# Delta attention and a mixture-of-experts MLP on one core: two chunks prepared together, weights loaded and decoded in another order

## The chip, the cores and the metric

The kernel is one program on one core of a Trainium2 chip. The core has TensorE (PE, matmuls and transposes), VectorE (DVE), ScalarE (ACT), GpSimd (POOL) and SyncE (SP, which only issues DMAs here), and 16 DMA engines that move data between HBM (DRAM) and the on-chip memory (SBUF). The metric is the device time of one execution in microseconds (us).

## The reference

Three stages follow one another. 32 heads (4 batches of 8) of a delta rule over 768 steps with head size 48; a squared-ReLU MLP whose weights are float64; and eight experts, of which each of the 3072 rows takes the one that scores best. Cut to what is computed:

```python
# q, k, v (4, 8, 768, 48), beta (4, 8, 768), float32
k_n = k / (np.linalg.norm(k, axis=-1, keepdims=True) + 1e-06)
for t in range(S):                      # 768 steps
    y[:, :, t] = np.einsum('bhd,bhde->bhe', q[:, :, t], state)
    v_old = np.einsum('bhde,bhd->bhe', state, k_n[:, :, t])
    state = state + beta_t * np.einsum('bhd,bhe->bhde', k_n[:, :, t], v_t - v_old)
x = y.transpose(0, 2, 1, 3).reshape(3072, 384)
h = np.maximum(x @ w_in, 0.0)           # w_in  384 x 2048, float64
x = (h * h @ w_out).astype(np.float32)  # w_out 2048 x 384, float64
expert_idx = np.argmax(x @ w_gate, axis=1)           # 8 experts
out[mask] = gate_w[mask] * (np.maximum(x[mask] @ w1[e], 0.0) @ w2[e])   # F = 1024
```

## The kernel before

**Phase 1** goes through the sequence in 12 chunks of 64 tokens (CH). For a chunk c, `pre(c)` loads k and q into the staging tiles st, transposes them into kq (in chunk 1 with matmuls against the identity, in all others with VectorE's block transpose, L359), forms the Gram matrices k k^T and k q^T on TensorE (L370, L371), and sends the key part through DRAM to lay it out anew: gd is written to dg (ScalarE's DMA queue) and read back as gl (SP's queue, L401). From gl come the norms (L440 and the lines behind it), and then a forward substitution inverts one 32x32 triangle per head and half chunk, 31 steps of a multiply (L482) and a subtract (L487). VectorE does each step in two interleaved halves, so that neighbouring instructions do not wait for each other: 120 instructions a chunk. The inverse pt goes out as dt and comes back as tt (L494, L502), again through DRAM.

`chain(c)` then advances the state: u steps (u = tt times the values vz, L547), z steps (what the state already holds is subtracted from vz, L540), y steps (the outputs, written as a high and a low part into xt, L580 and L581), and `s_step`, the update of the state.

The MLP of a chunk is eight units. `l1_unit` is 18 matmuls of 256 columns (L632, two blocks of nine), then ReLU (L636), square, and a split into a high and a low part (the low part on GpSimd, L640). `l2_unit` (L653) runs two units behind it (LAG). `route` picks the experts for the chunk's 256 rows and writes the rows into xs_d. **Phase 2** is the experts, slot by slot, with weights of their own; the change does not touch it.

**The float64 weights** w_in and w_out reach the kernel as pairs of int32 words, lo and hi. They are 14 raw tiles: six of w_in (rawi; 128 rows by 1024 values) and eight of w_out (rawo; 128 by 2 by 384 values), in the order: the three for w_in's first half, two of w_out, the three for w_in's second half, six of w_out. Each is decoded in two halves to float32 in the tile wt: VectorE shifts the exponent and mantissa bits (L141), puts in the sign (L142) and the top bits of lo (L148). The exponent fits float32 only if a value is not too small, so smaller ones are made zero: the hi word loses its sign and is compared with a bound. `DEC` says for each tile where: "b" strips the sign on VectorE (L146), "a" on ScalarE (L144), and both then compare and multiply on VectorE (L153); "s" does it all on ScalarE and GpSimd. At the end the float32 tile is split into high and low parts: a cast on ScalarE (L122) and a subtraction on GpSimd (L123).

**What sets the order.** Every engine works through its instructions in the order in which the code writes them; there is no scheduler. `pre`, `chain`, `update` and `load_weights` are generators, and each `yield` ends a step. Before the main loop the string `ramp` says which step comes next, letter by letter: A a step of chunk 0's `pre`, P one of chunk 1's, C one of chunk 0's `chain`, W a step of the weight decode, L a weight's loads on SP's queue, G the same on GpSimd's, D and E matmuls without a use, Z zeros written to DRAM, B, V, I and q the loads of beta, v and the next k and q. In the main loop every unit has two slots, 16 a chunk, and the tables PRE, CHAIN, LWAT and ROUTE_AT name the slot behind which a step is written:

```python
for n, (c, i) in enumerate(units):
    ...
    pend.append((c, i, l1_unit(c, i)))
    step_bg(NU * c + 2 * i)
    if len(pend) > LAG:
        a = pend.pop(0)
        l2_unit(*a)
    ...
    step_bg(NU * c + 2 * i + 1)
```

By these tables chunk 1's `pre` and `chain`, and the decode of most weights (LWAT), are written into chunk 0's units. `l1_unit` and `l2_unit` call for a weight step themselves if a weight that they need is not there yet.

## Time and profile before

| | |
|---|---|
| median of 3 runs | 1094.23 us (1093.82 to 1100.34) |
| the profiled execution | 1106.22 us, its span 1104.5 us |
| mean granted TensorE clock of that execution | 0.926 of full speed |
| busy, share of the span | TensorE 84%, VectorE 65%, ScalarE 46%, GpSimd 35% |
| first ReLU of chunk 0, 1, 2, 3 | 108.8, 208.3, 274.9, 328.3 us |

The span runs from the first to the last instruction. Busy is the time in which an engine had an instruction at work, issue of DMAs not counted. A stretch of the table's last row lasts from one chunk's first ReLU to the next one's; twelve such marks cut phase 1 into its chunks.

### The profile page before, as it was taken

How to read it: one execution, taken by the hardware profiler on the slowest of the kernel's cores; microseconds unless marked ns; L12 is line 12 of the kernel's file. 1: busy time of each engine (PE TensorE's matmuls, PEld its weight loads, DVE VectorE, ACT ScalarE, POOL GpSimd, SP SyncE). 2: the span in 40 equal slices, each digit the busy share in tenths (PEclk: the TensorE clock that was granted, in tenths of full speed). 3: DMA queues.
4: the chain of work that ended last, by engine and by line, in shares of the span. 5: the costliest groups of instructions: out<-in, count | busy, mean ns of one | idle time of the engine just before them, and what ended most of it. 6: DMA issues, size and time to landing. Idle time of an engine off the chain costs nothing.

```text
span 1104.5 us, 29012 instructions
## 1 busy us (share of the span) xinstructions
...
## 2 busy tenths in 40 slices
...
GB/s 123 117 160 78 127 70 153 12 33 69 61 72 35 76 49 86 35 75 47 84 41 78 48 82 43 42 36 114 131 130 132 258 164 176 222 179 147 215 206 131
DMA packets 284254, 114.22 MB, mean 103 GB/s; under 512 B 252829, under 2 KB 271330, under 8 KB 283712
## 3 DMA queue, kind: packets, MB, share of 16 engines
...
## 4 chain that ended last, share of the span: by engine, by line
PE 54%; DVE 20%; DMA 12%; issue 5%; SPq 4%; ACT 3%; POOL 0%; DVEq 0%; ACTq 0%; POOLq 0%
PE h L632 13%; PE x L653 11%; PE h L1003 6%; PE y L1015 5%; DVE tmp L482 5%; DVE pt L487 4%; PE h L1025 3%; PE y L1035 3%; DVE kq L359 2%; DVE wt L148 2%; DMA dt<-pt 2%; PE u L547 2%; PE wa L1035 2%; DVE wt L142 1%; DMA rawi<-in_moe_w_in_dram 1%
## 5 line engine op out<-in xcount | busy, mean ns | idle before, releaser
L632 PE MATMUL h<-xt,win 128*128 128x256 f32 x1728 | 250.2, 301 | 27.2 <-ACT r L636 11.1
L632 PEld LDWEIGHTS h<-xt,win 128*128 128x128 f32 x1728 | 232.4, 205 | 39.6 <-ACT r L636 11.8
L653 PE MATMUL x<-wout,gt 128*128 128x384 f32 x1152 | 224.8, 343 | 8.1 <-ACT wout L122 5.0
L653 PEld LDWEIGHTS x<-wout,gt 128*128 128x128 f32 x1152 | 198.7, 190 | 14.7 <-ACT wout L122 5.4
L640 POOL TENSOR_TENSOR gt<-r,gt 128x512 fp32r<-128x512 f32 x88 | 114.5, 1301 | 270.3 <-PE x L653 103.2
L482 DVE TENSOR_TENSOR tmp<-pt,gl 128x31 f32<-128x31 f32 (+4 forms) x720 | 153.6, 252 | 3.1 <-DVE pt L487 1.2
L487 DVE TENSOR_TENSOR pt<-pt,tmp 128x31 f32<-128x31 f32 (+4 forms) x720 | 142.8, 237 | 0.8
L636 ACT ACTIVATE r<-h 128x512 f32<-128x512 f32 x96 | 57.4, 598 | 168.1 <-PE h L632 139.3
L917 DVE TENSOR_TENSOR ew<-raw,ew 128x768 fp32r<-128x768 f32 (+1 forms) x98 | 102.5, 1070 | 15.2 <-ACT ew L916 12.7
L379 POOL TENSOR_TENSOR kq<-kq,qmask 64x256 f32<-64x256 f32 x96 | 73.2, 762 | 66.8 <-ACT kq L378 39.4
L916 ACT CAST ew<-raw 128x768 fp32r<-128x768 f32 (+1 forms) x98 | 87.5, 924 | 7.6 <-DMA raw<-in_moe_w_dram 7.6
L1003 PE MATMUL h<-xgT,ew 128*128 128x256 f32 x648 | 83.6, 284 | 7.1 <-issue 6.2
L1003 PEld LDWEIGHTS h<-xgT,ew 128*128 128x128 f32 x648 | 80.5, 191 | 9.5 <-issue 8.6
L1015 PE MATMUL y<-ew,ht 128*128 128x384 f32 x432 | 85.3, 344 | 0.1
...
L370 PE MATMUL gm<-kq 48*64 48x128 f32 (+1 forms) x416 | 60.3, 295 | 21.9 <-DVE kq L359 12.6
L1015 PEld LDWEIGHTS y<-ew,ht 128*128 128x128 f32 x432 | 74.4, 190 | 0.6 <-DVE ht L1007 0.4
L370 PEld LDWEIGHTS gm<-kq 48*64 48x64 f32 x416 | 47.3, 154 | 28.7 <-DVE kq L359 14.5
L359 DVE STREAM_TRANSPOSE kq<-st 64x512 f32<-64x512 f32 x88 | 62.1, 706 | 8.7 <-DMA st<-in_q_dram 7.1
L371 PE MATMUL gm<-kq 48*64 48x128 f32 (+1 forms) x416 | 58.2, 294 | 9.9 <-DVE kq L359 7.6
L1007 DVE SCALAR_TENSOR_TENSOR ht<-h,ht 128x512 fp32r<-128x512 f32 x36 | 24.8, 688 | 61.7 <-ACT ht L1006 53.2
L550 ACT COPY sw<-u 32x384 f32<-32x384 f32 x96 | 45.1, 470 | 41.4 <-PE u L547 39.4
...
## 6 DMA issues: line engine op xcount, KB each, us to landing
...
```

The lines of the kernel that those rows point to most:

```text
L359: nc.vector.transpose(out=kqs[hf][r, x, :, i * CH:(i + 1) * CH].rearrange("p r (u t) -> p r u t", u=2), in_=st[i][r, hf * HP:(hf + 1) * HP],)
L370: nc.tensor.matmul(gm[64:128, j, c0:c1], kq[0:D, 0, r, 0:CH], kq[0:D, 0, r, c0:c1], start=True, stop=True)
L379: nc.gpsimd.tensor_tensor(out=kq[h, x, rs, CH:P], in0=kq[h, x, rs, CH:P], in1=qmask[h].unsqueeze(1).to_broadcast([64, 4, CH]), op=ALU.mult,)
L482: eng.tensor_tensor(out=tv, in0=pt[:, js, s:s + 1].to_broadcast([P, m, n]), in1=gl[:, s:s + 1, s + 1:32].to_broadcast([P, m, n]), op=ALU.mult,
L487: eng.tensor_tensor(out=pt[:, js, s + 1:32], in0=pt[:, js, s + 1:32], in1=tv, op=ALU.subtract)
L632: nc.tensor.matmul(h[:, f2], win_t[kk, half][:, wl, f0:f0 + P], xt[:, xl, kk], start=(n == 0), stop=(n == 3 * KD - 1))
L640: eng.tensor_tensor(out=gt[:, 1], in0=r, in1=gt[:, 0], op=ALU.subtract)
L653: nc.tensor.matmul(x2_t[c][t], gt[:, gl_, f2, ts_], wout_t[i][:, wl, f2], start=(f == 0 and n == 0), stop=(f == NF - 1 and n == 2),)
L916: nc.scalar.copy(dst[:, 0], raw)
L917: nc.vector.tensor_tensor(out=dst[:, 1], in0=raw, in1=dst[:, 0], op=ALU.subtract)
L1003: nc.tensor.matmul(h[:, f2], a[kk][:, wl, f * P:f * P + P], xgT[:, xl, kk, 0:SLOT], start=(n == 0), stop=(n == 3 * KD - 1))
L1015: nc.tensor.matmul(y, ht[:, hl, f2, ts_], b[i][:, wl, f2], start=(f == 0 and n == 0), stop=(f == NF2 - 1 and n == 2),)
```

## The change

**One substitution for chunks 0 and 1.** `pre` is cut into `front` (transposes, Gram matrices of the keys, the way to gl) and `solve` (norms and substitution). `solve((0, 1))` runs the substitution of both chunks together: the two instructions that stand side by side are now chunk 0's and chunk 1's, each over all rows of its triangle, instead of the two halves of one chunk's. `front(0)` and `front(1)` both run ahead of it. The part of the Gram matrices that needs q is a generator of its own, `queries`, with its mask on VectorE. Chunk 1's gl lies in a buffer of xt. Chunks 2 to 11 keep the interleaved halves.

**Transposes.** Chunks 0, 1 and 2 are transposed on TensorE (`turn_in`), and the halves are copied from PSUM by ScalarE and, for x = 1, by VectorE. q of chunks 0 and 1 is staged in buffers of gt.

**Weights.** The decode is three steps of VectorE (shift, sign, low bits). Ahead of it, `lift` multiplies the hi words, read as float32, by 2 to the power of 8 - 119 on ScalarE, in place; this moves the exponent into range and makes small values zero. The weights are 2 to the 8 too large then, and the ReLU and the copy to xr take it out with their scale. The lift of a weight is written one weight ahead of its decode. The list `NEED` names the unit before which each weight is to be ready. The steps of the decode that do not fit ahead of the main loop follow it, in chunk 0's slots.

**Queues.** On SP's queue, weight 0 follows the keys of chunks 0 and 1, the other weights follow gl of both chunks, and none is loaded by GpSimd any more. GpSimd's queue takes q, v and beta of chunks 0 and 1 and half of chunk 0's tt. Chunk 1's CHAIN and chunk 2's PRE now follow the tables of all later chunks. The diff, cut to its core:

```diff
-    DEC="absbbbbabbabbb",
-    ramp="DLLqLLDBWDAAVIDWAWWAWAAAAADLZPAPPAPPPAAACAAAAWAAAWAAPEGWEWWWLLPDPPCPPPGCLCPPPPDCPPPPCPCCPPWWWCWWLGD",
+    ramp="KkqBiVMvLAPAPWaWWAPWaaaaSpWWLLLLLZCSSSSSSSSSSSSSSSSSppppSEEEEEWWWCEEWWWCEEWWWWCEEWWWWCCx",
...
+    NEED=(0, 0, 0, 0, 1, 1, 2.5, 4, 5.5, 7, 8.5, 10, 12, 14),
...
-    TR="dpdddddddddd",
-    WT="ggggrrrrrrrrrr",
+    TR="pppddddddddd",
+    WT="rgrgrgrrrrrrrr",
...
+    LIFT = 8 if wide else 0
+
+    def lift(raw):
+        hf = raw.rearrange("p (f two) -> p f two", two=2)[:, :, 1].bitcast(F32)
+        nc.scalar.activation(hf, hf, AF.Copy, scale=2.0 ** (LIFT - 119))
+
+    def decode(raw, wt):
         pair = raw.rearrange("p (f two) -> p f two", two=2)
         lo, hi = pair[:, :, 0], pair[:, :, 1]
...
-        nc.vector.tensor_scalar(wt, hi, 3, 0x3FFFFFF8, op0=ALU.logical_shift_left, op1=ALU.bitwise_and)
-        nc.vector.scalar_tensor_tensor(wt, hi, -0x40000000, wt, op0=ALU.bitwise_and, op1=ALU.bitwise_or)
-        if way in "ap":
-            nc.scalar.activation(hf, hf, AF.Abs)
-        elif way == "b":
-            nc.vector.tensor_scalar(hi, hi, 0x7FFFFFFF, None, op0=ALU.bitwise_and)
-        yield
+        nc.vector.tensor_scalar(wt, hi, 3, None, op0=ALU.logical_shift_left)
+        nc.vector.scalar_tensor_tensor(wt, hi, -0x80000000, wt, op0=ALU.bitwise_and, op1=ALU.bitwise_or)
         nc.vector.scalar_tensor_tensor(wt, lo, 29, wt, op0=ALU.logical_shift_right, op1=ALU.bitwise_or)
-        if way == "p":
-            nc.gpsimd.tensor_scalar(hf, hf, TINY, None, op0=ALU.is_ge)
-            nc.gpsimd.tensor_tensor(out=wf, in0=wf, in1=hf, op=ALU.mult)
-        elif way != "s":
-            nc.vector.scalar_tensor_tensor(wf, hf, TINY, wf, op0=ALU.is_ge, op1=ALU.mult)
...
+    def load_weights():
+        lifts(0)
+        yield
+        for n, (half, j) in enumerate(order):
+            if n:
+                lifts(n + 1)
+                yield
+            m, ris = halves(n)
...
+                if wide:
+                    decode(ri, wt[:, 0:m])
...
+                yield
...
+            for i in range(2):
+                split(t, i, wf[i])
+            yield
+            if n == 0:
+                lifts(1)
                 yield
...
+        vt, eng = vz[c % 2], (nc.gpsimd if c < 2 else nc.sync)
...
+                (nc.gpsimd if c < 2 and i else nc.sync).dma_start(out=tv[r0:r0 + 64], in_=head_view(a, par, c * CH, CH))
...
+    def turn_in(c, i):
+        kqs = kqb[c % 2]
+        src = src_t[c, i]
+        for g in range(4):
+            tp = ps_a.tile([P, 4, P], F32, tag="a", name="tp")[0:64]
+            hf, js = g // 2, slice(4 * (g % 2), 4 * (g % 2) + 4)
+            for j in range(4):
+                r = 4 * g + j
+                nc.tensor.transpose(tp[:, j], src[:, r * D:r * D + 64], ident)
+            for x in range(2):
+                to, by = kqs[hf][64 * x:64 * x + 64, x, js, i * CH:(i + 1) * CH], tp[:, :, 64 * x:64 * x + 64]
+                if (c < 2 and i == 0 or c == 2) and x:
+                    nc.vector.tensor_copy(to, by)
+                else:
+                    nc.scalar.copy(to, by)
...
+    def solve(cs):
+        w = 32 * len(cs)
+        gls = [gl_t.pop(c) for c in cs]
...
+        both = len(cs) > 1
...
+            for h in range(2):
+                js, m = (slice(0, nj), nj) if both else (slice(h, nj, 2), (nj + 1 - h) // 2)
+                if m:
+                    ops.append((gls[h * both], pts[h * both], js, m, tmp[:, h, 0:m * n].rearrange("p (a b) -> p a b", a=m)))
...
+                        (nc.gpsimd if c == 0 and x else nc.sync).dma_start(out=tt[r0:r0 + 32, u], in_=dtr[hf, x, u])
...
-        nc.scalar.activation(r, h, AF.Relu)
+        nc.scalar.activation(r, h, AF.Relu, scale=2.0 ** -LIFT)
...
-            nc.scalar.copy(xr, x2p[t])
+            nc.scalar.activation(xr, x2p[t], AF.Copy, scale=2.0 ** -LIFT)
...
-                nc.sync.dma_start(out=bl[r0:r0 + 32], in_=bf[:, :, u, :])
+                nc.gpsimd.dma_start(out=bl[r0:r0 + 32], in_=bf[:, :, u, :])
...
+    step = {"A": f0, "P": f1, "S": p01, "C": ch, "u": update(0), "W": lw, "a": qs[0], "p": qs[1]}
```

What the instructions of three places look like before and after, in the program's order; the number behind a tile's name is its buffer's.

**VectorE, the substitution, the fifth of the 31 steps and half of the sixth.** tmp is the product, pt the inverse that grows. Before, one chunk (pt_375, gl_283), each instruction over every second row:

```order
L482 TENSOR_TENSOR tmp_393<-pt_375,gl_283 128x54
L482 TENSOR_TENSOR tmp_393<-pt_375,gl_283 128x27
L487 TENSOR_TENSOR pt_375<-pt_375,tmp_393 128x2x27
L487 TENSOR_TENSOR pt_375<-pt_375,tmp_393 128x27
L482 TENSOR_TENSOR tmp_393<-pt_375,gl_283 128x52
L482 TENSOR_TENSOR tmp_393<-pt_375,gl_283 128x26
```

After, chunk 0 (pt_455, gl_400) and chunk 1 (pt_456, gl_403):

```order
L503 TENSOR_TENSOR tmp_566<-pt_455,gl_400 128x81
L503 TENSOR_TENSOR tmp_566<-pt_456,gl_403 128x81
L508 TENSOR_TENSOR pt_455<-pt_455,tmp_566 128x3x27
L508 TENSOR_TENSOR pt_456<-pt_456,tmp_566 128x3x27
L503 TENSOR_TENSOR tmp_566<-pt_455,gl_400 128x78
L503 TENSOR_TENSOR tmp_566<-pt_456,gl_403 128x78
```

The same places hold instructions of 81 and 78 elements for each of two chunks, where they held 54 and 27, 52 and 26 for one.

**VectorE, the decode of a w_out tile.** Before, five instructions for a half, two halves:

```order
L141 TENSOR_SCALAR wt_1153<-rawo 128x384
L142 SCALAR_TENSOR_TENSOR wt_1153<-rawo,wt_1153 128x384
L146 TENSOR_SCALAR rawo<-rawo 128x384
L148 SCALAR_TENSOR_TENSOR wt_1153<-rawo,wt_1153 128x384
L153 SCALAR_TENSOR_TENSOR wt_1153<-rawo,wt_1153 128x384
```

After, from the last step ahead of a decode that stands in the ramp (a z step) over the two halves of the tile:

```order
L570 TENSOR_TENSOR vz_134<-vz_134,z 128x384
L130 TENSOR_SCALAR wt_901<-rawo 128x384
L131 SCALAR_TENSOR_TENSOR wt_901<-rawo,wt_901 128x384
L132 SCALAR_TENSOR_TENSOR wt_901<-rawo,wt_901 128x384
L130 TENSOR_SCALAR wt_901<-rawo 128x384
L131 SCALAR_TENSOR_TENSOR wt_901<-rawo,wt_901 128x384
L132 SCALAR_TENSOR_TENSOR wt_901<-rawo,wt_901 128x384
```

L146 and L153 are gone from VectorE, and nothing writes to rawo there.

**SP's queue around dt, the way of pt through DRAM.** Before, from the loads of chunk 1's v (vz_141) and k (ktok) to chunk 1's gl:

```order
L314 DMA vz_141<-in_v_dram 32x8x32
L295 DMA ktok_643<-in_k_dram 64x16x48 x2
L494 DMA dt_226<-pt_375 1024x1x32 x2
L502 DMA tt_722<-dt_226 32x8x32 x8
L401 DMA gl_731<-dg_445 64x1024 x2
L178 DMA rawo<-in_moe_w_out_dram 128x768 x2
```

After, from weight 0 to chunk 0's tt:

```order
L157 DMA rawi<-in_moe_w_in_dram 32x2048 x4
L415 DMA gl_400<-dg_207 64x1024 x2
L415 DMA gl_403<-dg_237 64x1024 x2
L157 DMA rawi<-in_moe_w_in_dram 32x2048 x4
L157 DMA rawi<-in_moe_w_in_dram 16x2048 x8
L157 DMA rawo<-in_moe_w_out_dram 128x2x768 x2
L157 DMA rawi<-in_moe_w_in_dram 32x2048 x8
L157 DMA rawi<-in_moe_w_in_dram 16x2048 x8
L273 DMA ktok_563<-in_k_dram 64x16x48 x2
L518 DMA dt_691<-pt_455 1024x1x32 x2
L518 DMA dt_694<-pt_456 1024x1x32 x2
L528 DMA tt_697<-dt_691 32x8x32 x4
```

Seven weights and ktok stand between gl of both chunks and dt; before, ktok alone stood right ahead of it, and chunk 1's gl behind tt.

## Rows read from the trace of the kernel before

**Rows 1.** Busy time of each engine (instructions) by stretch, PEclk, DMA share, GB/s.

```profile
0.00:108.80 108.80, 44.29 (x750) 36.50 (x754) 78.69 (x322) 31.99 (x79) 39.06 (x64) 0.76 0.71 119
108.80:208.30 99.50, 59.82 (x730) 54.36 (x731) 88.54 (x126) 39.55 (x86) 51.11 (x52) 0.73 0.50 99
208.30:274.90 66.60, 57.44 (x816) 51.46 (x815) 52.31 (x227) 29.13 (x66) 18.81 (x19) 0.88 0.31 45
274.90:328.30 53.40, 51.75 (x800) 46.94 (x800) 33.77 (x140) 28.70 (x64) 18.20 (x18) 0.99 0.46 70
328.30:755.60 427.30, 401.86 (x6253) 371.05 (x6252) 290.40 (x1276) 209.94 (x459) 139.92 (x136) 0.98 0.36 56
```

**Rows 2.** Timeline of ScalarE: chunk 0's and chunk 3's first ReLU.

```profile
108.77 0.60 ACT L636 ACTIVATE r<-h 128x512 f32<-128x512 f32 x1 [1.39 <-PE h L632]
...
328.34 0.60 ACT L636 ACTIVATE r<-h 128x512 f32<-128x512 f32 x1 [2.91 <-PE h L632]
```

**Rows 3.** Chain that ended last, start and length, from 143 us.

```profile
143.09 1.37 DVE rawi L146
144.46 1.69 DVE wt L148
```

**Rows 4.** Groups by line and shape, first 210 us.

```profile
L632 PE MATMUL h<-xt,win 128*128 128x256 f32 x162 | 31.4, 365 | 18.7 <-ACT r L636 11.1 <-DVE xt L581 4.4 <-ACT win L122 1.9
...
L146 DVE TENSOR_SCALAR rawo<-rawo 128x384 int32<-128x384 int32 x14 | 13.4, 960 | 0.5
L153 DVE SCALAR_TENSOR_TENSOR wt<-rawo,wt 128x384 f32<-128x384 f32 x16 | 11.8, 738 | 0.7
L359 DVE STREAM_TRANSPOSE kq<-st 64x512 f32<-64x512 f32 x16 | 11.3, 705 | 7.5 <-DMA st<-in_q_dram 7.1
...
L153 DVE SCALAR_TENSOR_TENSOR wt<-rawi,wt 128x512 f32<-128x512 f32 x10 | 7.3, 726 | 0.6
...
L146 DVE TENSOR_SCALAR rawi<-rawi 128x512 int32<-128x512 int32 x6 | 5.0, 834 | 0.2
...
L144 ACT ACTIVATE rawi<-rawi 128x512 f32<-128x512 f32 x4 | 2.7, 684 | 14.4 <-DVE wt L142 14.4
```

**Rows 5.** VectorE on the tile wt, first 210 us.

```profile
0.00:210.00 210.00, 78.88 (x110) 0.75 0.60 109
```

**Rows 6.** Timeline of VectorE: five places in chunk 0's substitution.

```profile
37.81 0.19 DVE L482 TENSOR_TENSOR tmp<-pt,gl 128x31 f32<-128x31 f32 x1
...
39.75 0.29 DVE L482 TENSOR_TENSOR tmp<-pt,gl 128x29 f32<-128x29 f32 x2
39.98 0.29 DVE L487 TENSOR_TENSOR pt<-pt,tmp 128x29 f32<-128x29 f32 x2
...
45.29 0.36 DVE L482 TENSOR_TENSOR tmp<-pt,gl 128x72 f32<-128x72 f32 x2
45.56 0.35 DVE L487 TENSOR_TENSOR pt<-pt,tmp 128x72 f32<-128x72 f32 x2
```

**Rows 7.** Chain that ended last, first 140 us.

```profile
31.45 0.27 ACT s L440
...
65.62 0.58 SPq L494
...
71.62 5.36 DMA tt<-dt
...
112.24 13.03 DMA rawi<-in_moe_w_in_dram
```

**Rows 8.** Timeline of TensorE: chunk 0's first u step and first layer-1 matmul.

```profile
81.71 1.58 PE L547 MATMUL u<-vz,tt 32*32 32x48 f32 x64
...
96.51 0.38 PE L632 MATMUL h<-xt,win 128*128 128x256 f32 x1 [0.46 <-ACT xt L580]
```

**Rows 9.** Timeline of GpSimd: two of its DMA issues.

```profile
36.73 0.83 POOL L788 DMA_DIRECT2D wg<-in_moe_w_gate_dram  x1
...
38.57 0.62 POOL L793 DMA_DIRECT2D xs_d<-zrow  x1
```

315 lines of the change are left out of this document (148 added, 167 removed).

## The prediction

> **What bounds the kernel now.** I read the stretches first. Cut at the first ReLU of each chunk, a settled chunk takes 53.4 us: TensorE is busy 51.75 of chunk 2's 53.4, VectorE 33.8, and the eight chunks from 328.3 on average the same 427.3/8 [rows 1]. The change leaves that part and all that follows alone, so what it can win lies before chunk 3's first ReLU, at 328.34 [rows 2]. Three stretches lie there: 108.8 us up to chunk 0's first ReLU, 99.5 us for chunk 0 and 66.6 us for chunk 1. In chunk 0's 99.5 us TensorE is busy 59.8 and VectorE 88.5, so VectorE sets the pace. The chain of waits says with what: the weight decode, whose 128x384 steps are long at this place (L146 1.37 us, L148 1.69) [rows 3]. The groups by line and shape say what one step costs on average there [rows 4]. In the first stretch nothing is full, VectorE 78.7 of 108.8 and the DMA engines 0.71 [rows 1]: it is a path of dependent steps, and I price it as a path.
>
> **The decode.** 28 weight halves are decoded. L146 (the sign stripped on VectorE) is 13.4 + 5.0 us and L153 (tiny values flushed) 11.8 + 7.3 us [rows 4]: together 37.5 us leave VectorE. The three steps that stay write wt, as L153 does; VectorE works on wt for 78.9 us in 110 instructions [rows 5], and without L153's 26 that is 59.8 us for 84, or 2.14 us a half. These are means with GpSimd at work beside them, as it will be again. In exchange ScalarE lifts all 28 halves, at L144's 0.684 us at most 19 us [rows 4]. Its own queue is in order, so a lift that waits for its load holds up every ReLU behind it; that is the second rival.
>
> **One substitution for two chunks.** The 31 steps are 120 instructions a chunk now, in two interleaved halves, and 124 for both chunks afterwards, each on a whole triangle row. Two instructions of 29 elements take 0.23 us from start to start and the two of 72 and 54 take 0.27 [rows 6]: 0.04 us for 68 more elements, so some 0.6 ns an element over 0.098 us an instruction. Both chunks have 4 x 2856 elements, which gives 124 x 0.098 + 11424 x 0.0006 = 19 us; were all of the longer pair's 0.27 us for 126 elements to grow with the elements, it would be 24. I take 20, and 3 more for the stalls beside GpSimd. From the square root (31.45) to the first step (37.81) it is 6.4 us [rows 6, 7]; a second scaled gl and two more clears add some 3. Were the solve to start at 31.5 as before, it would end at 31.5 + 9.4 + 23 = 64, against 65.6 for chunk 0 alone now [rows 7]. So chunk 1's solve costs the first stretch almost nothing.
>
> **The path to the first ReLU.** Then pt goes out and comes back as tt. Now that takes from 65.62 to the landing of tt at 71.62 + 5.36 = 77.0, 11.4 us [rows 7]. By VectorE alone tt would be there at 64 + 11.4 = 75.4. But dt now stands in SP's queue behind seven more weights and ktok. By the shapes in the code 13.3 MB are to move before it: 7.9 of weights 0 to 7, 2.4 of k, q and v, 1.6 of dg and gl, 0.9 of zeros, 0.5 of beta and ktok. The first 108.8 us move 119 GB/s at a share of 0.71, 168 GB/s while busy [rows 1], which makes 79 us; the large packets of weights 6 and 7 with ktok (2.5 MB) took 13.0 us [rows 7], 191 GB/s, which makes 70. I take 73 and 8 more for dt and tt, so tt at 81 (bounds 75 and 89). From u's first matmul to the first layer-1 matmul it is 96.51 - 81.71 = 14.8 us now [rows 8]; decoding weights 3 and 4 lies in that stretch and fits beside u, the copies and y, and I leave it at 14 to 15. A layer-1 unit of 18 matmuls takes 31.4/9 = 3.5 us at that clock [rows 4]. Now 12.3 us pass between the first layer-1 matmul and the first ReLU, because weights 1 and 2 are not split; afterwards they are decoded while tt is in flight. First ReLU: 81 + 14.3 + 3.5 = 98.8 against 108.8. **Gain 10** (2 to 16).
>
> **Chunk 0.** Nine weights are left, 18 halves x 2.14 = 38.5 us of VectorE. A settled chunk's other work is 33.8 [rows 1]. Of it the transposes of one chunk go (8 x 0.705 = 5.6 [rows 4]) and eight copies from PSUM come (no row; between 0.3 and 0.6, by the 0.29 to 0.36 of small steps [rows 6] and the 0.705 of a transpose; I take 0.35, 2.8 us), and 9 us of chunk 2's solve fall into chunk 1's stretch by the table. That is 60 us. At the share that VectorE reaches now, 88.5 of 99.5, it takes 67; without any idle time 60. TensorE has 51.75 less the two second-layer units that lag, plus 32 transposes: about as much, at a clock that was 0.73 here [rows 1] and may stay under 1. I take 64. **Gain 35.5** (27 to 40).
>
> **Chunk 1.** A settled 53.4, and 9 us more VectorE work, which fits in the 19.6 us that VectorE idles: 55. **Gain 11.6** (6 to 13).
>
> **What costs nothing.** GpSimd takes over q, v and beta of chunks 0 and 1 and half of chunk 0's tt: 48 DMAs stand ahead of the first u step in its queue. An issue of 128 pieces took 0.62 us there and one of 384 took 0.83 [rows 9], some 1 ns a piece, so the four of 1024 pieces take about 1.5 and all 48 some 36 us, with 6 of memsets and splits 42: hidden until 81. If that cover is gone, see the third rival. The relu's and the copy's scale ride on instructions that are there. TensorE's 64 transposes for chunks 0 and 1 replace 64 smaller matmuls and VectorE's transposes, while TensorE mostly waits.
>
> **Sum.** 10 + 35.5 + 11.6 = 57 us off the profiled execution's 1106.2 (its span is 1104.5) is 1049. The median of the three runs, 1094.2, lies 12 us below that execution; the gain is in the same stretch for both, so I forecast **1037**.
>
> **Rivals.** First: the DMA engines rule the start. If they move no more than the 119 GB/s that the first stretch averages, 13.3 MB take 112 us, tt is there at 120 and the first ReLU comes at 138, 29 us later than now; chunks 0 and 1 still give 47, net 18, so 1076. For it: the share is 0.71 with VectorE waiting; against it: by the code's shapes k and q of chunk 0 come in pieces of 64 and 128 bytes now and of 192 afterwards, weights 0 to 2 in pieces of 4 KB and then of 8. Second: chunk 0 stays uneven, because lifts, splits and ReLUs share ScalarE's queue. Its 39.6 us of chunk 0 [rows 1] become some 52: lifts and splits of the remaining weights (about 20) on a settled chunk's 28.7, and 3 of copies. If every unit waits 2 us for a lift, chunk 0 takes 80 and the time is 1053. Third, the other side: GpSimd's queue. All of chunk 0 hangs on its tt, behind those 48 DMAs. At x us each tt lands at 48x + 10; up to 1.5 us nothing is lost, and from 2.7 us on (tt at 140) the whole gain is gone. At 3.1 us tt lands at 159, 78 us late, and the time is 1115. Both issues in rows 9 were made while VectorE ran the substitution, and took 0.62 and 0.83.
>
> The Trainium skill speaks for this rival: its page "SBUF — State Buffer" says under "SBUF: two separate sides" that a DMA issued by GpSimd waits for its descriptors while VectorE holds the port they share, and under "A bandwidth-pool intuition that's wrong (but worth ruling out)" gives 3.1 us in place of 0.62. By that figure the time would be the 1115 above. The trace disagrees here, with 0.62 and 0.83 us beside a busy VectorE [rows 9].
>
> **How the numbers follow.** Forecast, 1020 to 1050: 0.60. ScalarE's queue, about 1053: 0.15. DMA, about 1076: 0.10. GpSimd, 1100 and more: 0.04. Better than forecast, with tt at 75 and chunk 0 bound by TensorE at 55, about 1018 or less: 0.09. Little or nothing, because a wait that I don't see takes the place: 0.02. The range is 1013 to 1066: it takes in the first two and the better case, and leaves out DMA and what is slower. Within 1% (1083 to 1105) is about what a measurement of this kernel can't tell from no change. Faster by more: the forecast, ScalarE, the better case and most of the DMA case, 0.92; within 1%: 0.04; slower: 0.04.
>
> **What would show it.** In the new profile: the joint substitution ends before 70 us; tt lands between 75 and 89, with dt issued late if the weights hold it; the first ReLU comes at 93 to 105, chunk 1's 60 to 70 us later, chunk 3's between 258 and 282, and from there to the end nothing changes; VectorE's busy time falls by 40 to 60 us, ScalarE's rises by 5 to 15. I am wrong if chunk 0's stretch stays over 80 us with VectorE under 75% busy, which would say that the decode was not what paced it, or if GpSimd's DMA issues at the start take over 1.5 us each.

## The result and the profile after

| | before | after |
|---|---|---|
| median of 4 runs | 1097.06 us (1093.82 to 1100.34) | 1053.30 us (1052.08 to 1055.59) |
| the profiled execution, span | 1106.22, 1104.5 us | 1052.59, 1050.8 us |
| first ReLU of chunks 0, 1, 2, 3 | 108.8, 208.3, 274.9, 328.3 us | 101.5, 175.4, 227.0, 282.4 us |

The ratio is 0.9603, with a 95% interval of 0.9562 to 0.9645: 43.8 us faster by the medians, where 57 were forecast. The predicted time, 1037 us, is 16 us below the measured one, inside the stated range.

Busy time by stretch after the change, cut at the same marks as [rows 1] (from:to, length, then busy time and instructions of TensorE's matmuls and weight loads, VectorE, ScalarE and GpSimd, then clock, DMA share and GB/s):

```profile
0.00:101.50 101.50, 50.44 (x736) 36.28 (x740) 69.87 (x235) 28.84 (x68) 43.43 (x70) 0.71 0.94 194
101.50:175.40 73.90, 54.07 (x778) 48.44 (x776) 62.01 (x126) 45.60 (x105) 41.05 (x36) 0.85 0.26 43
175.40:227.00 51.60, 50.77 (x800) 46.02 (x799) 33.84 (x147) 28.79 (x64) 17.31 (x18) 1.00 0.37 58
227.00:282.40 55.40, 52.07 (x801) 47.77 (x800) 40.49 (x177) 28.87 (x65) 19.24 (x19) 0.95 0.41 66
282.40:708.70 426.30, 402.73 (x6252) 373.54 (x6252) 291.60 (x1264) 210.09 (x459) 139.84 (x136) 0.97 0.35 56
```

The marks are the ReLUs that answer to [rows 2]; the timeline of ScalarE:

```profile
101.50 0.60 ACT L668 ACTIVATE r<-h 128x512 f32<-128x512 f32 x1 [6.14 <-PE h L664]
...
282.38 0.60 ACT L668 ACTIVATE r<-h 128x512 f32<-128x512 f32 x1 [7.41 <-PE h L664]
```

Read against [rows 1], stretch by stretch:

| stretch | before | after | gain | forecast |
|---|---|---|---|---|
| to chunk 0's first ReLU | 108.8 | 101.5 | 7.3 | 10 |
| chunk 0 | 99.5 | 73.9 | 25.6 | 35.5 |
| chunk 1 | 66.6 | 51.6 | 15.0 | 11.6 |
| chunk 2 | 53.4 | 55.4 | -2.0 | 0 |
| chunks 3 to 10 | 427.3 | 426.3 | 1.0 | 0 |
| from chunk 11's first ReLU to the end | 348.9 | 342.1 | 6.8 | 0 |

The four stretches that the change touches give 45.9 us where 57 were forecast. The last row is chunk 11 and phase 2, which the change all but leaves alone: its length differed from profile to profile in all the kernels below, between 341.0 and 349.8 us, and the 6.8 us in that row are of that kind. Chunks 3 to 10 took between 420.5 and 431.4 us there.

What happens at the start shows on SP's queue (start, time until the last issue of the row, queue, line, transfer and count):

```profile
54.10 17.58 SPq L157 DMA_DIRECT2D rawi<-in_moe_w_in_dram  x10
71.73 1.35 SPq L273 DMA_DIRECT2D ktok<-in_k_dram  x2
73.18 4.35 SPq L518 DMA_DIRECT2D dt<-pt  x4
78.44 5.78 SPq L528 DMA_DIRECT2D tt<-dt  x12
```

and on VectorE, where the first and the last steps of the joint substitution answer to [rows 6]:

```profile
40.30 0.29 DVE L503 TENSOR_TENSOR tmp<-pt,gl 128x31 f32<-128x31 f32 x2
...
60.77 0.30 DVE L508 TENSOR_TENSOR pt<-pt,tmp 128x16 f32<-128x16 f32 x2
```

The inverse is ready at 61.1, but its transfer is issued at 73.2, behind ten pieces of weights that SP's queue gave out between 54.1 and 71.7: the 73 of the prediction, and a wait of 12 us.

In chunk 0 the decode is the reading to make. VectorE on the tile wt, in the first two stretches:

```profile
0.00:101.50 101.50, 22.41 (x36) 4.37 (x8) 10.07 (x8) 0.71 0.94 194
101.50:175.40 73.90, 42.71 (x48) 9.88 (x20) 23.41 (x20) 0.85 0.26 43
```

48 instructions are 16 halves, so a half costs 2.67 us in chunk 0, against 2.14 forecast from [rows 5]; in the first stretch it is 22.41/12 = 1.87. Undisturbed, the three steps of a 128x512 half take 0.42, 0.69 and 0.69 us (at 70 us). VectorE's busy time in chunk 0, 62.0, is nevertheless near the 60 of the prediction. But the stretch is 73.9 and not 64: VectorE stands idle for 11.9 us of it, most of them in one wait at the start, behind ScalarE's half of the copies of chunk 2's transposes.

```profile
108.68 1.41 DVE L329 COPY kq<-tp 64x256 f32<-64x256 f32 x4 [7.75 <-ACT kq L331]
```

TensorE, busy for 54.1 us, stands still in two large holes. TensorE's timeline, with the idle time before the instruction and what ended it:

```profile
149.53 2.97 PE L566 MATMUL z<-sw,kq 96*32 96x48 f32 x64 [7.42 <-ACT sw L580]
...
169.21 0.58 PE L664 MATMUL h<-xt,win 128*128 128x256 f32 x1 [5.74 <-ACT xt L610]
```

Both wait for a small copy on ScalarE, and this is what stands ahead of the copies there:

```profile
148.06 0.93 ACT L116 CAST wout<-wt 128x384 fp32r<-128x384 f32 x2 [2.17 <-DVE wt L132]
149.00 1.95 ACT L580 COPY sw<-u 32x384 f32<-32x384 f32 x4
...
167.86 0.92 ACT L116 CAST wout<-wt 128x384 fp32r<-128x384 f32 x2 [6.61 <-DVE wt L132]
168.69 0.47 ACT L610 CAST xt<-y 128x384 fp32r<-128x384 f32 x1
```

A cast that waits for VectorE's decode keeps the next chunk's small copies (of its state, L580, and of its outputs, L610) waiting behind it, and TensorE with them.

### The profile page after: what moved, and what is told of

The parts are those of the page before. It is cut to its first block, busy times and chain, and to the rows that moved or that the text cites. A ratio compares the mean times of both kernels' runs of the same rounds, so it can differ in the third digit from the quotient of the medians.

```text
span 1050.8 us, 28874 instructions
## 1 busy us (share of the span) xinstructions
PE 921.1 (88%) x11416; PEld 857.7 (82%) x11416; DVE 673.4 (64%) x2234; ACT 511.6 (49%) x1025; POOL 382.4 (36%) x388
## 5 line engine op out<-in xcount | busy, mean ns | idle before, releaser
L664 PE MATMUL h<-xt,win 128*128 128x256 f32 x1728 | 245.0, 297 | 26.5 <-DVE xt L611 15.7
L664 PEld LDWEIGHTS h<-xt,win 128*128 128x128 f32 x1728 | 226.8, 201 | 35.2 <-DVE xt L611 18.1
L672 POOL TENSOR_TENSOR gt<-r,gt 128x512 fp32r<-128x512 f32 x88 | 114.1, 1296 | 277.7 <-ACT gt L670 101.4
L685 PEld LDWEIGHTS x<-wout,gt 128*128 128x128 f32 x1152 | 201.6, 193 | 9.1 <-issue 3.7
L503 DVE TENSOR_TENSOR tmp<-pt,gl 128x60 f32<-128x60 f32 (+37 forms) x662 | 146.4, 259 | 2.4 <-DVE tmp L503 0.4
L508 DVE TENSOR_TENSOR pt<-pt,tmp 128x60 f32<-128x60 f32 (+37 forms) x662 | 133.0, 239 | 0.7
L942 ACT CAST ew<-raw 128x768 fp32r<-128x768 f32 (+1 forms) x98 | 87.6, 923 | 11.9 <-DMA raw<-in_moe_w_dram 11.9
L1041 PEld LDWEIGHTS y<-ew,ht 128*128 128x128 f32 x432 | 74.8, 191 | 0.1
L390 POOL TENSOR_TENSOR kq<-kq,qmask 64x256 f32<-64x256 f32 x80 | 60.1, 751 | 35.6 <-issue 18.8
L580 ACT COPY sw<-u 32x384 f32<-32x384 f32 x96 | 45.1, 470 | 38.1 <-PE u L577 36.2
L669 ACT ACTIVATE r<-r 128x512 f32<-128x512 f32 x96 | 60.7, 632 | 3.0
L670 ACT CAST gt<-r 128x512 fp32r<-128x512 f32 x96 | 59.6, 621 | 5.1 <-ACT r L669 0.4
L1069 POOL DMA_INDIRECT out_dram<-yo,ids x30 | 33.5, 1117 | 70.0 <-DMA out_dram<-yo,ids 21.1
L381 PE MATMUL gm<-kq 48*64 48x128 f32 (+1 forms) x384 | 49.1, 268 | 6.4 <-DVE kq L370 6.2
```

Of the source, the lines that this page charges most:

```text
L390: nc.gpsimd.tensor_tensor(out=kq[h, x, rs, CH:P], in0=kq[h, x, rs, CH:P], in1=qmask[h].unsqueeze(1).to_broadcast([64, 4, CH]), op=ALU.mult,)
L503: nc.vector.tensor_tensor(out=tv, in0=pt[:, js, s:s + 1].to_broadcast([P, m, n]), in1=gl[:, s:s + 1, s + 1:32].to_broadcast([P, m, n]), op ...
L508: nc.vector.tensor_tensor(out=pt[:, js, s + 1:32], in0=pt[:, js, s + 1:32], in1=tv, op=ALU.subtract)
L664: nc.tensor.matmul(h[:, f2], win_t[kk, half][:, wl, f0:f0 + P], xt[:, xl, kk], start=(n == 0), stop=(n == 3 * KD - 1))
L669: nc.scalar.activation(r, r, AF.Square)
L670: nc.scalar.copy(gt[:, 0], r)
```

## The experiments

Four theories went in. **V**: VectorE's decode paces chunk 0. **P**: the gain comes from preparing both chunks ahead, not from the decode. **Q**: ScalarE's queue, worked through in order, paces chunk 0. **D**: SP's queue of weights sets tt. The medians of before differ by chip (1095.5 to 1103.5 us), so the ratio to before on the same chip is what compares; first ReLU and chunks are from each kernel's profile.

| kernel | ratio, 95% interval | median | first ReLU | chunk 0 | chunk 1 |
|---|---|---|---|---|---|
| changed kernel | 0.9603, 0.9562 to 0.9645 | 1053.3 | 101.5 | 73.9 | 51.6 |
| e1_old_decode | 0.9747, 0.9669 to 0.9824 | 1067.5 | 103.1 | 87.5 | 56.0 |
| e2_new_decode_alone | 1.0019, 0.9974 to 1.0063 | 1098.9 | 124.8 | 76.8 | 69.3 |
| e3_weights_behind_tt | 0.9514, 0.9434 to 0.9594 | 1045.1 | 92.4 | 73.7 | 52.0 |
| e4_no_gpsimd_split | 0.9455, 0.9378 to 0.9533 | 1038.1 | 101.4 | 63.0 | 57.6 |
| e5_lift_in_place | 0.9947, 0.9911 to 0.9984 | 1094.2 | 106.2 | 92.2 | 65.5 |
| e6_copies_on_scalar | 0.9681, 0.9626 to 0.9736 | 1067.6 | 105.1 | 74.8 | 52.0 |
| e7_weights_needed_later | 0.9583, 0.9515 to 0.9651 | 1057.3 | 104.9 | 70.4 | 57.8 |
| e8_two_substitutions | 0.9705, 0.9641 to 0.9769 | 1068.8 | 112.9 | 74.1 | 54.6 |
| e9_casts_ahead | 0.9600, 0.9507 to 0.9692 | 1061.3 | 107.0 | 72.1 | 56.3 |
| e10_all_three | 0.9515, 0.9431 to 0.9600 | 1051.0 | 92.9 | 73.1 | 53.4 |
| e11_low_part_unread | 0.9639, 0.9583 to 0.9695 | 1057.1 | 101.7 | 74.0 | 54.4 |
| e12_masks_on_vector | 0.9553, 0.9494 to 0.9611 | 1045.7 | 91.1 | 77.1 | 54.6 |

### The change without its decode, and the decode without the rest

**e1_old_decode.** On the changed kernel:

```diff
-    LIFT = 8 if wide else 0
+    LIFT = 0
...
-        nc.scalar.activation(hf, hf, AF.Copy, scale=2.0 ** (LIFT - 119))
...
+        nc.vector.tensor_scalar(wt, hi, 3, 0x3FFFFFF8, op0=ALU.logical_shift_left, op1=ALU.bitwise_and)
+        nc.vector.scalar_tensor_tensor(wt, hi, -0x40000000, wt, op0=ALU.bitwise_and, op1=ALU.bitwise_or)
+        nc.vector.tensor_scalar(hi, hi, 0x7FFFFFFF, None, op0=ALU.bitwise_and)
         nc.vector.scalar_tensor_tensor(wt, lo, 29, wt, op0=ALU.logical_shift_right, op1=ALU.bitwise_or)
+        nc.vector.scalar_tensor_tensor(wt.bitcast(F32), hi.bitcast(F32), TINY, wt.bitcast(F32), op0=ALU.is_ge, op1=ALU.mult)
```

> The changed kernel with the old decode: five steps on VectorE for every weight half (sign stripped and tiny values flushed there), no lift on ScalarE, no scale in the ReLU. Theory V (chunk 0 is paced by VectorE's decode): 12 halves stand ahead of the first ReLU and 16 behind it, each longer by 1.6 to 1.7 us; the first ReLU comes 5 to 8 us later than 101.5, chunk 0 takes 93 to 100 us in place of 73.9, and the time is 1078 to 1088 us. Theory P (what the change won came from preparing both chunks ahead and from the order, not from the decode): chunk 0 stays under 82 and the time under 1063. Theory Q (ScalarE's queue, in order, with the lifts in it, paces chunk 0): without lifts chunk 0 gets no longer, 1048 to 1056.

Busy time by stretch, first and second:

```profile
0.00:103.10 103.10, 51.13 (x736) 36.65 (x740) 80.68 (x257) 22.66 (x57) 43.82 (x70) 0.73 0.93 195
103.10:190.60 87.50, 58.36 (x778) 51.95 (x775) 79.36 (x160) 38.01 (x89) 40.94 (x36) 0.78 0.20 31
```

VectorE is busy 17.4 us longer in chunk 0 (79.4 against 62.0), the chunk takes 13.6 us longer and the next one 4.4. The time lies between the bands of V and P; Q in this form is out, for ScalarE lost its lifts and nothing got shorter. The first ReLU, which V had 5 to 8 us later, came 1.6 later, though VectorE's work ahead of it grew by 10.8 us (69.9 to 80.7): the start hangs little on the decode. The rest of the change without the decode gives 2.5% (by the interval 1.8 to 3.3), and the decode on top of it 1.4%.

**e2_new_decode_alone.** On the kernel before; decode and scales as in the change, and in `weight`:

```diff
+        if n == 0:
+            lift(0)
+        lift(n + 1)
         raw = raw_t.pop(n)
```

> The kernel before with nothing changed but the decode: three steps, the lift one weight ahead, the scales in ReLU and copy. Theory V: VectorE's 88.5 us in chunk 0 fall by 20 to 28, chunk 0's 99.5 us to 72 to 80, the first ReLU moves by less than 5, the time is 1069 to 1077 us against 1097. Theory P: chunk 1's preparation, a chain of dependent steps, still fills chunk 0; chunk 0 stays over 90 and the time is 1087 to 1097.

Busy time by stretch, and ScalarE's lift of weight 3:

```profile
0.00:124.80 124.80, 41.85 (x746) 34.51 (x750) 73.10 (x319) 32.06 (x80) 38.45 (x67) 0.76 0.70 122
124.80:201.60 76.80, 52.99 (x731) 48.51 (x732) 63.66 (x81) 45.51 (x99) 46.49 (x42) 0.83 0.48 100
```

```profile
94.84 0.55 ACT L141 ACTIVATE rawo<-rawo 128x384 f32<-128x384 f32 x1 [22.05 <-DMA rawo<-in_moe_w_out_dram]
```

Chunk 0 has the length that theory V gave it, 76.8 for 99.5. But the first ReLU comes 16 us later, because a lift waited 22 us for its weight in ScalarE's queue, with the square root and the state's copies behind it, so the chunk ends, at chunk 1's first ReLU, only 6.7 us earlier (201.6 for 208.3). Alone, the new decode wins nothing.

**e5_lift_in_place.** As e2, with the lift inside `decode`, right ahead of its first step:

```diff
+        nc.scalar.activation(hf, hf, AF.Copy, scale=2.0 ** (LIFT - 119))
         nc.vector.tensor_scalar(wt, hi, 3, None, op0=ALU.logical_shift_left)
```

> The kernel before with the three-step decode, as in e2, but each half's lift written right ahead of its own decode and not one weight ahead; nothing else is changed. In e2 chunk 0 fell from 99.5 to 76.8 us, and the first ReLU came 16 us later, because a lift in ScalarE's queue waited 22 us for weight 3. If that wait is the whole cause: the first ReLU comes at 106 to 112, chunk 0 takes 74 to 82, and the time is 1070 to 1080 us against 1095. If lifts as such hold up ScalarE wherever they stand (theory Q): the first ReLU stays later than 115 or chunk 0 over 85, and the time is 1085 to 1097.

```profile
0.00:106.20 106.20, 43.59 (x746) 36.28 (x750) 69.04 (x314) 30.99 (x77) 36.18 (x62) 0.59 0.70 122
106.20:198.40 92.20, 58.97 (x729) 53.67 (x730) 61.42 (x88) 47.25 (x102) 49.69 (x52) 0.74 0.54 107
```

Two of VectorE's waits for a lift:

```profile
110.69 1.78 DVE L138 TENSOR_SCALAR wt<-rawo 128x384 int32<-128x384 int32 x1 [3.10 <-ACT rawo L137]
116.54 1.08 DVE L138 TENSOR_SCALAR wt<-rawo 128x384 int32<-128x384 int32 x1 [2.89 <-ACT rawo L137]
```

The start is as expected (106.2), chunk 0 is not: it and the time lie in the bands of Q. VectorE's busy time in it fell by 27 us, 88.5 to 61.4 [rows 1], and the chunk by 7.3. So VectorE's work alone does not pace it. In place of the work came waits: VectorE waited 13 times for a lift in this chunk, 23.1 us in all, and never in e2, where 61 to 64 us of the same work took 76.8 us and not 92.2. Part of that difference is where chunk 0 is taken to begin: its end, chunk 1's first ReLU, comes at 198.4 here and at 201.6 in e2. Either way theory V in its plain form falls.

### The start

**e3_weights_behind_tt.** One edit of the table: the loads of weights 5 to 7 are written behind dt and tt.

```diff
-    ramp="KkqBiVMvLAPAPWaWWAPWaaaaSpWWLLLLLZCSSSSSSSSSSSSSSSSSSppppSEEEEEWWWCEEWWWCEEWWWWCEEWWWWCCx",
+    ramp="KkqBiVMvLAPAPWaWWAPWaaaaSpWWLLZCSSSSSSSSSSSSSSSSSSLLLppppSEEEEEWWWCEEWWWCEEWWWWCEEWWWWCCx",
```

> The changed kernel with the loads of weights 5, 6 and 7 written behind dt and tt on SP's queue instead of ahead. If the queue of weights holds dt (theory D): the substitution ends at 61, dt is issued by 63 in place of 73.2, tt has landed by 73 in place of 83, the first ReLU comes at 90 to 93 in place of 101.5, and the time is 1042 to 1046 us. If tt is not what the first ReLU waits for (decode of weights 3 and 4, the state chain on ScalarE), or if the three weights then come too late, the first ReLU stays within 3 us and the time at 1050 to 1056.

SP's queue, and busy time by stretch:

```profile
42.08 12.06 SPq L273 DMA_DIRECT2D ktok<-in_k_dram  x2
61.61 2.88 SPq L518 DMA_DIRECT2D dt<-pt  x4
65.50 5.79 SPq L528 DMA_DIRECT2D tt<-dt  x12
71.34 8.51 SPq L157 DMA_DIRECT2D rawi<-in_moe_w_in_dram  x13
```

```profile
0.00:92.40 92.40, 49.57 (x740) 35.14 (x744) 73.44 (x235) 29.20 (x68) 44.35 (x70) 0.76 0.91 161
92.40:166.10 73.70, 52.84 (x778) 47.13 (x773) 61.79 (x124) 45.60 (x104) 41.11 (x36) 0.88 0.45 108
```

Theory D holds: dt is issued at 61.6 in place of 73.2, the first ReLU comes 9.1 us earlier, chunk 0 keeps its length, and the three weights are still early enough. The two later kernels with this edit, e10 and e12, repeat it (92.9 and 91.1).

**e8_two_substitutions.** On e3:

```diff
-    ramp="KkqBiVMvLAPAPWaWWAPWaaaaSpWWLLZCSSSSSSSSSSSSSSSSSSLLLppppSEEEEEWWWCEEWWWCEEWWWWCEEWWWWCCx",
+    ramp="KkqBiVMvLAPAPWaWWAPWaaaaSpWWLLZCSSSSSSSSSSSSSSSSSLLLSSSSSSSSSSSSSSSSSppppEEEEEWWWCEEWWWCEEWWWWCEEWWWWCCx",
...
-    f0, f1, p01, ch = front(0), front(1), solve((0, 1)), chain(0)
...
+    f0, f1, p01, ch = front(0), front(1), two(), chain(0)
...
+    def two():
+        yield from solve((0,))
+        yield from solve((1,))
```

> The kernel of e3 (weights 5 to 7 behind tt, 1045 us) with two substitutions one after the other, chunk 0's and then chunk 1's, each in its two interleaved halves, in place of the joint one; dt and tt of chunk 0 are issued after the first. By the prediction's price the joint one takes 20 us for both and a single one some 15 to 17: the first ends near 56 and tt lands 4 to 6 us earlier than in e3, but VectorE is at the second until 74 to 78, and the decode of weights 1 and 2 and the first z step come behind it. First ReLU 93 to 100 in place of 92.4, time 1046 to 1053. If tt alone sets the first ReLU: 86 to 90, time 1039 to 1043. If the joint substitution is what the change lives on: 105 or later, over 1057.

VectorE, the wait in the middle of the first substitution:

```profile
53.29 0.96 DVE L491 TENSOR_TENSOR vz<-vz,ncol 128x768 f32<-128x768 f32 x1 [10.30 <-ACT ncol L489]
```

and ScalarE around it:

```profile
52.01 1.19 ACT L125 ACTIVATE rawi<-rawi 128x512 f32<-128x512 f32 x2 [11.21 <-DMA rawo<-in_moe_w_out_dram]
53.10 0.15 ACT L489 COPY ncol<-nps 128x16 f32<-128x16 f32 x1
```

112.9 against e3's 92.4 (and 92.9 in e10, on the same chip) is, by the number, the third case of the expectation, but 10.3 us of it are something that I had not seen in my own edit: a single substitution scales vz by the norms at its tenth step, and the copy of the norms stood on ScalarE behind a lift that waited 11.2 us for its weight. The joint one does the norms after its last step. Without the 10.3 the first ReLU would be near 102.6, an estimate between the first case and the third, and about 10 us are left for the joint substitution itself. So the run bears out that it is worth that much, and not cleanly.

### Chunk 0

**e4_no_gpsimd_split.** The subtraction that forms the weights' low part is left out:

```diff
-        nc.gpsimd.tensor_tensor(out=dst[:, 1, n], in0=raw, in1=dst[:, 0, n], op=ALU.subtract)
...
-                    nc.tensor.matmul(h[:, f2], win_t[kk, half][:, wl, f0:f0 + P], xt[:, xl, kk], start=(n == 0), stop=(n == 3 * KD - 1))
+                    nc.tensor.matmul(h[:, f2], win_t[kk, half][:, 0, f0:f0 + P], xt[:, xl, kk], start=(n == 0), stop=(n == 3 * KD - 1))
...
-                        x2_t[c][t], gt[:, gl_, f2, ts_], wout_t[i][:, wl, f2],
+                        x2_t[c][t], gt[:, gl_, f2, ts_], wout_t[i][:, 0, f2],
```

> The changed kernel without GpSimd's subtraction that forms the weights' low part; the matmuls that read the low part read the high part in its place, so the product is less exact. GpSimd loses 28 of its instructions of 1.1 to 1.3 us. Theory V with contention (GpSimd's own work beside a decode step stretches it): a half's decode in chunk 0 falls from 2.67 us to 2.1 or less, chunk 0 from 73.9 to 63 to 68, the time to 1043 to 1048. Theory Q (the casts and copies in ScalarE's queue pace it, whatever VectorE takes): decode at 2.67, time 1050 to 1056.

Busy time in chunk 0, of all instructions and then of those on wt:

```profile
101.40:164.40 63.00, 51.20 (x778) 46.37 (x775) 49.18 (x123) 45.35 (x105) 17.81 (x16) 0.91 0.34 62
```

```profile
101.40:164.40 63.00, 32.62 (x48) 9.87 (x20) 0.91 0.34 62
```

A half's decode falls to 32.62/16 = 2.04 us and chunk 0 by 10.9, as theory V with contention expected; chunk 1 gives 6 back. The time, 1038.1, is below the 1043 of that theory: by the ratios this kernel is some 16 us faster than the changed one, of which the two stretches show 4.9, and the rest is not placed. What this kernel leaves out is more than exactness: the high part stands in for the low one and counts twice, so h comes out about twice as large. The matmuls' number and shapes are the same.

**e11_low_part_unread.** Of e4 only what the matmuls read: GpSimd subtracts, and nothing on TensorE waits for it.

> The changed kernel in which GpSimd still forms the weights' low part, but no matmul reads it (they read the high part in its place, as in e4, so the product is less exact). GpSimd's work is that of the changed kernel; only TensorE's waits for it are gone. It splits what e4 won: chunk 0 there took 63.0 us in place of 73.9, at 2.04 us a half's decode in place of 2.67. If GpSimd's work beside VectorE stretches the decode (contention): 2.6 to 2.7 us a half as in the changed kernel, chunk 0 at 71 to 74, and 0.958 to 0.962 of the time before. If TensorE's waits for the low part are what e4 took away: chunk 0 at 63 to 66, and 0.945 to 0.950.

Chunk 0, all instructions and those on wt:

```profile
101.70:175.70 74.00, 51.92 (x777) 46.82 (x773) 63.20 (x128) 45.62 (x104) 41.09 (x36) 0.86 0.28 53
101.70:175.70 74.00, 43.84 (x50) 9.88 (x20) 23.45 (x20) 0.86 0.28 53
```

Chunk 0 stays at 74.0, and a half's decode at 2.63 us (43.84 for 50 steps, three to a half). What e4 took away is GpSimd's work itself, not TensorE's waits for it. How GpSimd's work reaches VectorE shows in one pair of rows of the changed kernel, VectorE's and GpSimd's (a subtraction for the ReLU's low part, of the same operation and size as those for w_in):

```profile
119.06 1.79 DVE L132 SCALAR_TENSOR_TENSOR wt<-rawi,wt 128x512 int32<-128x512 int32 x1
```

```profile
119.04 1.27 POOL L672 TENSOR_TENSOR gt<-r,gt 128x512 fp32r<-128x512 f32 x1 [0.56 <-ACT gt L670]
```

GpSimd starts 0.02 us earlier and is done at 120.31; VectorE's step, 0.69 us when undisturbed, is done at 120.85, 0.54 behind it. It waited out nearly the whole instruction. In e11 the same two instructions take 1.78 and 1.27 us, and VectorE's is again done 0.54 us behind.

**e6_copies_on_scalar.** VectorE stands idle for 7.8 us at the start of chunk 0 behind a copy of chunk 2's transposes; these copies go to ScalarE.

```diff
-                if (c < 2 and i == 0 or c == 2) and x:
+                if c < 2 and i == 0 and x:
```

> The changed kernel with the eight copies of chunk 2's transposes that VectorE makes moved to ScalarE; chunks 0 and 1 keep theirs. In the changed kernel VectorE stands idle for 7.8 us at the start of chunk 0, behind such a copy, with the decode of weight 6 next in its queue. Theory V (VectorE's queue paces chunk 0, its waits count in full): the idle time is gone, chunk 0 falls from 73.9 to 66 to 69 us, the time to 1045 to 1049. Theory Q (ScalarE's queue): 8 x 0.36 us more on ScalarE, chunk 0 gets 0 to 3 us longer, 1053 to 1057.

Busy time in chunk 0, and what VectorE does in the place of that wait:

```profile
105.10:179.90 74.80, 53.87 (x778) 47.69 (x771) 60.53 (x118) 49.25 (x113) 41.50 (x36) 0.86 0.27 44
```

```profile
110.46 1.27 DVE L130 TENSOR_SCALAR wt<-rawi 128x512 int32<-128x512 int32 x1 [5.65 <-POOL wout L117]
```

No gain in chunk 0, as Q expected: the next wait takes over at once, for a wt buffer that weight 4's cast and subtraction had still to read. (The first ReLU is 3.6 us later though the edit changes nothing ahead of it; e7, on the same chip, shows the same with 3.4.)

**e7_weights_needed_later.** The last six weights are written 1 to 2.5 slots later.

```diff
-    NEED=(0, 0, 0, 0, 1, 1, 2.5, 4, 5.5, 7, 8.5, 10, 12, 14),
+    NEED=(0, 0, 0, 0, 1, 1, 2.5, 4, 6.5, 8.5, 10.5, 12.5, 14.5, 16.5),
```

> The changed kernel with the decode of the last six weights written 1 to 2.5 slots later (their due slots 6.5, 8.5, 10.5, 12.5, 14.5 and 16.5 in place of 5.5, 7, 8.5, 10, 12 and 14), so that the last one falls into chunk 1, where VectorE stands idle for a third of the time. Theory Q (TensorE's two holes of 7.4 and 5.7 us come from casts in ScalarE's queue that wait for the decode, ahead of the copies of chunk 1's state): the holes shrink by 6 to 10 us, chunk 0 takes 64 to 68, the time is 1043 to 1047. Theory V (the sum of VectorE's work and waits sets the pace): only the work that leaves chunk 0 counts, 2 halves or 4 to 5 us, chunk 0 takes 68 to 71 and chunk 1 up to 2 more, the time is 1048 to 1052.

Chunk 0 falls by 3.5 us to 70.4, as V expected, but it began 3.4 us later: chunk 1's first ReLU stands where it stood, at 175.3 for 175.4. Chunk 1 rises by 6.2 to 57.8, more than either theory allowed. The two together are no shorter.

**e9_casts_ahead.** Five more weight steps ahead of the main loop:

```diff
-    ramp="KkqBiVMvLAPAPWaWWAPWaaaaSpWWLLLLLZCSSSSSSSSSSSSSSSSSSppppSEEEEEWWWCEEWWWCEEWWWWCEEWWWWCCx",
+    ramp="KkqBiVMvLAPAPWaWWAPWaaaaSpWWLLLLLZCSSSSSSSSSSSSSSSSSSppppSEEEEEWWWCEEWWWCEEWWWWCEEWWWWCCWWWWWx",
```

> The changed kernel with five more weight steps written ahead of the main loop: the casts of weights 4 and 5 and the lift of weight 6 now stand ahead of the first ReLU in ScalarE's queue, not behind it; VectorE's and TensorE's order is the same. In e6 VectorE, freed of its wait for chunk 2's copies, waited 5.7 us instead for the buffer that weight 4's cast and subtraction had still to read; that cast stood behind the first ReLU and the state's copies. Theory Q (ScalarE's order sets chunk 0's pace, through the lifts ahead of VectorE and the casts behind it): about 3 us of ScalarE work move out of chunk 0, which falls from 73.9 to 69 to 72 us, with the first ReLU at most 1 us later for this; the time is 1048 to 1052 by the ratio to the kernel before. Theory V (VectorE's own queue): its wait for chunk 2's copies stays as it is, 73 to 75 us, 1052 to 1055.

Chunk 0 falls by 1.8 us to 72.1, the end of Q's band, but the first ReLU comes 5.5 us later, where at most 1 was expected and e6 and e7 show some 3.5 on the same chip; the time, by the ratio of 0.9600, does not move.

**e10_all_three.** The edits of e3, e6 and e9 in one kernel.

> The edits of e3, e6 and e9 together: weights 5 to 7 behind tt, all of chunk 2's copies on ScalarE, the casts of weights 4 and 5 ahead of the first ReLU. e3's 9 us at the start should stay in full. In chunk 0 VectorE now has neither the wait for chunk 2's copies nor the wait for weight 4's buffer, and can decode weight 6 from the first ReLU on. Theory Q: chunk 0 at 66 to 69 us where e6 alone gave 74.8, the time 1037 to 1042. If the two waits only give way to the next one in the loop of lift, decode, cast and subtraction: chunk 0 at 72 to 75, and the time that of e3, 1043 to 1047.

```profile
92.90:166.00 73.10, 55.44 (x713) 48.70 (x714) 59.65 (x116) 46.20 (x107) 39.37 (x34) 0.83 0.44 107
```

```profile
104.35 0.43 DVE L130 TENSOR_SCALAR wt<-rawi 128x512 int32<-128x512 int32 x1 [6.05 <-POOL gt L672]
```

e3's 9 us stay, and chunk 0 does not move: with both waits gone VectorE waits 6.05 us for the next buffer of the ring that wt shares with the ReLU's r, here until GpSimd had read r. The second outcome of the expectation is the one that came.

**e12_masks_on_vector.** On e3:

```diff
-                if c1 == P and c < SCHED["QM"]:
+                if c1 == P and 2 < c < SCHED["QM"]:
```

> The kernel of e3 (weights 5 to 7 behind tt) with chunk 2's eight mask multiplies on VectorE, straight from PSUM, in place of a ScalarE copy and a GpSimd multiply each. In chunk 0 GpSimd loses 6.8 us of work, ScalarE 2.9, and VectorE gets 8 x 0.42 = 3.4 more. If GpSimd's work stretches VectorE's steps in proportion (18 us of stretch beside 41 us of GpSimd's work): 3 us less stretch and less in ScalarE's queue, chunk 0 falls from e3's 73.7 to 70 to 73, the time to 0.946 to 0.951 of before. If VectorE's own work is all that counts: 75 to 77, 0.952 to 0.955.

Chunk 0, all instructions and those on wt:

```profile
91.10:168.20 77.10, 56.32 (x777) 51.09 (x774) 57.19 (x135) 43.41 (x97) 32.78 (x28) 0.79 0.45 106
```

```profile
91.10:168.20 77.10, 34.43 (x48) 9.87 (x20) 22.02 (x20) 0.79 0.45 106
```

The decode falls from 2.67 to 2.15 us a half, far more than its share, and VectorE from 61.8 to 57.2 in all; yet chunk 0 gets 3.4 us longer. The numbers, 77.1 and 0.9553, lie at the end of the expectation's second side, but its reason, more work on VectorE, is not what happened. By their intervals the times of e3 and e12 can't be told apart. VectorE now waits for ScalarE and ScalarE for VectorE, turn by turn, at the copies of one Gram tile, and TensorE's hole ahead of the same z step is 8.4 us. A shorter decode did not shorten chunk 0 here.

## Why the prediction was right, and which terms were off

**The place and the direction** were right: everything that the change moves lies before chunk 3's first ReLU, and from there to the end the time is the same to within what those rows vary by.

**The path to the first ReLU**, forecast at 98.8 with tt at 81, came at 101.5. The substitution took 40.3 to 61.1, 20.8 us, for 20 plus 3. That dt would stand in SP's queue until about 73 was read correctly, and the first u matmul, which waits for tt, came at 80.5. From there to the first layer-1 matmul it took 14.9 us for 14.3, and from that one to the ReLU 6.1 for 3.5, which is where the 2.7 us went: the unit stood still 1.6 us for the low part of xt, at a granted clock of 0.58 of full speed.

```profile
80.53 0.33 PE L577 MATMUL u<-vz,tt 32*32 32x48 f32 x2 [9.64 <-DMA tt<-dt]
...
95.41 0.39 PE L664 MATMUL h<-xt,win 128*128 128x256 f32 x1 [1.31 <-ACT xt L610]
```

e3 shows that dt's place in the queue was the bound: with dt free at 61.6 the first ReLU moves by 9.1 us. The step "By VectorE alone tt would be there at 75.4" was thus the better half of the change, left unused.

**Chunk 0** is the term that failed: "I take 64", measured 73.9. The sum of VectorE's work behind it was nearly right (60 forecast, 62.0 measured), though by errors that partly cancel: 16 halves and not 18, at 2.67 us and not 2.14. The other 7.9 of the 9.9 us are VectorE's idle time, 11.9 where the 64 left 4. What was wrong was to carry "VectorE sets the pace" from the kernel before, whose chain runs through the decode [rows 3], over to the changed one, at a share of 94% (60 of 64). e5 took 27 us of VectorE's work out of chunk 0 and won 7; e6, e9 and e10 took away waits one after another and won 1.8 at most; e12 shortened the decode and lost 3.

What the traces show in its place is a loop through three engines: lift on ScalarE, decode on VectorE, cast on ScalarE, subtraction on GpSimd, and back over four shared buffers, with ScalarE's queue in between, in which the next chunk's copies wait behind the casts. That this loop as a whole sets the length is argued from these runs; no single run shows it. GpSimd's part of it is worth up to 10.9 us in chunk 0 (e4), and not by TensorE's waits (e11). How much of that is the stretched decode and how much the buffers that come free earlier stays open; e12 says that the first is not enough. Buffers of wt's own, which would have told the two apart, were not tried. TensorE's clock also has a part, and no run held it fixed: the 778 matmuls of chunk 0 (777 in e12's trace) are busy for 54.1 us at a granted clock of 0.85 of full speed in the changed kernel, 51.2 at 0.91 in e4 and 56.3 at 0.79 in e12.

**The second rival**, ScalarE's queue with chunk 0 at 80 and a time of 1053, was nearer to the truth than the forecast, and I gave it 0.15. That its time fits the measured 1053.3 is luck, for its chunk 0 is 6 us too long. It named lifts that wait for loads; in the changed kernel these are casts that wait for the decode. Where the loads come late, e2 shows the lifts doing just what the rival said, with 16 us.

**Chunk 1** came at 51.6 for 55 and chunk 2 at 55.4 for 53.4; the sum is off by 1.4.

**DMA rival.** The engines moved 194 GB/s in the first stretch, where the rival took 119 for their limit. At a share of 0.94 they were nearly full, but e3, at 0.91, has its first ReLU 9.1 us earlier: the order of the transfers counted.

**GpSimd's queue**, the slow rival, did not come. Its last issue ahead of tt, while VectorE ran the substitution, and the four for tt:

```profile
46.58 0.54 POOL L827 DMA_DIRECT2D g_d<-zrow  x1
78.97 2.35 POOL L528 DMA_DIRECT2D tt<-dt  x4 [31.86 <-DMA dt<-pt]
```

The issue beside the substitution took 0.54 us, and the queue had been waiting for 31.9 us when dt arrived. (Of the two issues of [rows 9] only the second was made during the substitution, whose first step is at 37.81 [rows 6]; the first was over at 37.56.) The Trainium skill, page "SBUF — State Buffer", section "Who interferes with whom", names VectorE's copies, casts and tensor_scalar as the operations that can take the shared ports, and says that tensor_tensor did not stall a DMA; the substitution is tensor_tensor throughout, and the trace agrees, with 0.54 us. I had cited the trap without that restriction.

**The signs named beforehand.** The substitution ended before 70 (61.1), the first ReLU lay between 93 and 105 (101.5), and VectorE's busy time fell from 719.3 to 673.4 us by the page, within 40 to 60. Chunk 1's first ReLU came 73.9 us after chunk 0's and not 60 to 70, chunk 3's at 282.4, just behind the 282 of the forecast, and ScalarE's busy time rose by 3.7 us only, 507.9 to 511.6, for 5 to 15.

**The median.** I took 12 us off for the difference between the profiled execution and the median, as if it were the same for both kernels. The changed kernel's profiled execution, 1052.6, lies 0.7 below its median. From the four-run median, 1097.1 - 45.9 would have been 1051.2, within 2.1 us of the measured time.

The best version that leaves nothing out is e3 (e10 is level with it): 0.9514 of before, against 0.9603 for the change. Their intervals overlap (0.9434 to 0.9594, 0.9562 to 0.9645), but the 9 us are seen at the same place in all three kernels that have the edit.
